# Turning the last 128 output columns of two matmuls in three of four token chunks

## The chip, the cores and the metric

One core of one Trainium2 chip. The metric is the device time of one execution in microseconds, here the median of three runs.

## The reference, cut to what matters

Two branches read the same x (2048 tokens of 640 features): a linear attention A and an MLP mixer B. They are mixed with a gate per token.

```python
o = num / den                                   # linear attention, 32 heads of 20
a = o.reshape(B, S, D) @ wo
x1 = x + hs                                     # hs: first MLP, shifted over tokens, @ w2
h2 = gelu(layernorm(x1) @ w3) @ w4              # w3: 640 x 1728, w4: 1728 x 640
b = x1 + h2
g = sigmoid((x * gate_w).sum(-1, keepdims=True))
return g * a + (1 - g) * b
```

With wo folded into the attention's key-value matrix (M, 640 x 640), the last stage is, for each token, g times (scaled query @ M), plus (1 - g) times (x1 + h @ w4), with h the result of the gelu.

## The kernel before, in words

The tokens are 16 tiles of 128 and four chunks of 512. The first stages make queries, keys, the gate, the key-value matrix M, and the first MLP (x_tok then holds x1). The last stages, around the change, are:

- **w3** (w3_group): per chunk 13 groups of 128 hidden features; each is five matmuls with 512 tokens moving into one bank of PSUM, and one gelu on ScalarE into h2T. The last 64 of the 1728 hidden features (w3_half) go to h2h, on partitions 0 to 63 for the even tiles and 64 to 127 for the odd.
- **attention tile** (a_tile, lines 1071 to 1080): POOL writes (1 - g) times x_tok of a tile into a slot of abx (four slots); TensorE multiplies the tile's scaled query, stationary, by M, moving: five matmuls of 512 output columns into one bank and five of 128 into the next; VectorE adds g times that to abx.
- **w4** per chunk: w4_half (lines 1084 to 1106) opens the accumulation with the 64 left hidden features, for the four tiles of the chunk at once, each pair of tiles side by side on the two halves of the array's rows. w4_tile (lines 1108 to 1131) then adds 13 matmuls of 512 columns and 13 of 128 per tile, with a 128 x 128 block of h2T stationary each time. VectorE then adds (1 - g) times PSUM to abx and writes x_tok: a 512-wide and a 128-wide instruction (both at line 652, the helper stt). out_tiles stores finished tiles.

PSUM has eight banks of 512 fp32 columns. `bank()` (line 527) picks one free bank, `pair()` (line 544) one of the four fixed pairs (0, 1), (2, 3), (4, 5), (6, 7) in which neither bank is held; each takes the one that its plan frees earliest. w4_half holds six banks, three whole pairs: four for the tiles' 512 columns and two for their tails. A bank leaves the hold when its tile's last group has been recorded.

The order of the work on each engine is made when the kernel is built: a planner (`_Items.run`, line 349) takes items from streams, each with a duration, dependencies and lags, and records the operations of the item that may start first. Every recorded operation waits on semaphores for the reads and writes before it (`_Sched.op`, line 216). So the order of instructions is fixed and what happens at run time is only waiting. Near the change the plan puts attention tile t + 4 behind w4 tile t, the w3 groups of the next chunk but one behind the four tiles, and the query scaling of tiles 12 to 15 on VectorE into chunk 0. Helpers record most operations, so many instructions have one line: L613 is a matmul group, L635 a multiply by a scalar, L652 a sum of a scaled input, L669 an activation, L282 a transposing DMA on SP.

Of the kernel before, what the change touches and what calls it, by code (L numbers as in the profile page):

```python
# [5 lines left out]
BF16 = mybir.dt.bfloat16  # L6
F32 = mybir.dt.float32
ACTF = mybir.ActivationFunctionType
ALU = mybir.AluOpType
# [41 lines left out]
class _Sched:  # L51
# [161 lines left out]
            if any(r.lo < 0 for r in lst):  # L213
                self.recs[space] = [r for r in lst if r.lo >= 0]

    def op(self, eng, fn, reads=(), writes=(), deps=(), cost=500.0):
        d, touched, newrecs, banks = self._collect(eng, reads, writes)
        d.extend(deps)
        waits = self._waits(eng, d)
        self.cnt[eng] += 1  # L220
        sem = "c:" + eng
        vc = dict(self.know[eng])
        ev = _Ev(sem, self.cnt[eng], vc)
        self._commit(ev, touched, newrecs, banks, eng)
        self.prog[eng].append((waits, fn, sem))
        self.seq.append((eng, waits, cost, sem, ev.val, 0))
        self.oplog.append((eng, ev.val, self.cur_item, waits))
        self.stats["ops"] += 1
        self.stats["waits"] += len(waits)
        return ev  # L230
# [199 lines left out]
def _build(nc, A_x, A_wqkv, A_wo, B_w1, B_w2, B_w3, B_w4, gate_w, out, dbg=None, stop=None):  # L430
# [113 lines left out]
    def pair():  # L544
        best = None
        for k_ in range(4):
            q_ = (bank_rr[0] // 2 + k_) % 4
            tf = 0.0
            ok = True
            for b in (2 * q_, 2 * q_ + 1):  # L550
                if b in bank_pend or b in bank_hold:
                    ok = False
                lk = sch.locks.get(b)
                if lk is not None:
                    tf = max(tf, sch.ev_time.get((lk[1].sem, lk[1].val), 1e18))
            if ok and (best is None or tf < best[0]):
                best = (tf, 2 * q_)
        b = best[1]
        bank_rr[0] = b + 2
        bank_pend.update((b, b + 1))  # L560
        return b
# [8 lines left out]
    def nfree(ap):  # L570
        n = 1
        for d_ in ap.shape[1:]:
            n *= d_
        return n
# [20 lines left out]
            cost = 150.0 + 1.2 * n  # L595
        return sch.op("pool", fn, reads, writes, cost=cost)

    def pe(fn, reads, writes, cost=500.0):
        for w_ in writes:
            sp_, rl = sch.rects(w_)  # L600
            if sp_ == "ps":
                for (_p0, _p1, lo, hi) in rl:
                    for b in range(lo // PS_BANK, (hi - 1) // PS_BANK + 1):
                        bank_pend.discard(b)
        return sch.op("pe", fn, reads, writes, cost=cost)

    def mm_group(out_ap, pairs, reads_extra=()):
        n = len(pairs)

        def fn(e, out_ap=out_ap, pairs=pairs, n=n):  # L610
            ins = None
            for i, (l, r) in enumerate(pairs):
                ins = e.matmul(out_ap, l, r, start=(i == 0), stop=(i == n - 1))  # L613
            return ins
        reads = [a for p in pairs for a in p] + list(reads_extra)
        return pe(fn, reads, [out_ap], cost=n * (max(nfree(pairs[0][1]), 24) * 0.4167 + 2.5))
# [11 lines left out]
    def ts(engf, out_ap, in_ap, s1, s2, op0, op1, extra_reads=()):  # L628
        rd = [in_ap] + [a for a in (s1, s2) if not isinstance(a, (int, float)) and a is not None] + list(extra_reads)
        cost = None  # L630
        if engf is pool:
            cost = 190.0 + 1.15 * nfree(out_ap)
        elif in_ap.dtype == BF16 and out_ap.dtype == BF16 and not in_psum(in_ap):
            cost = 65.0 + nfree(out_ap) / 3.84
        return engf(lambda e: e.tensor_scalar(out_ap, in_ap, s1, s2, op0, op1), rd, [out_ap], cost=cost)  # L635
# [431 lines left out]
        sch.dma("sp", pqnT[:, :, 128 * t:128 * (t + 1)], pq_tok[:, t, :], "trn%d" % slot("trn", 4), transpose=True)  # L1067

    abx_slot = {}

    def a_tile(t):
        sa = slot("abx", 4)
        abx_slot[t] = sa
        tag_set("abx", sa, t)
        ts(pool, abx[:, sa, :], x_tok[:, t, :], stg[:, 3, t:t + 1], 0.0, ALU.mult, ALU.add)
        tok = slice(128 * t, 128 * (t + 1))
        b = pair()
        mm_group(ps[:, b, 0:512], [(pqnT[:, j, tok], M_sb[:, j, 0:512]) for j in range(KD)])
        mm_group(ps[:, b + 1, 0:128], [(pqnT[:, j, tok], M_sb[:, j, 512:D]) for j in range(KD)])
        stt(abx[:, sa, :], psf[:, 512 * b:512 * b + D], stg[:, 2, t:t + 1], abx[:, sa, :], ALU.mult, ALU.add)  # L1080

    w4_banks = {}

    def w4_half(t):
        sl = (t // 4) % 2
        tag_chk("h2T", sl, t // 4)
        b0, b2, bt = pair(), pair(), pair()
        tiles = [((b0, b2)[i // 2] + i % 2, bt + i % 2, 128 * (i // 2)) for i in range(4)]
        for i in range(4):
            w4_banks[t + i] = tiles[i]  # L1090
        bank_hold.update((b0, b0 + 1, b2, b2 + 1, bt, bt + 1))

        def fn(e):
            ins = None
            for pr in range(2):
                for par, tail in ((0, False), (1, False), (0, True), (1, True)):
                    rows = slice(64 * par, 64 * par + 64)
                    bm, bs, q0 = tiles[2 * pr + par]
                    l = h2h[rows, t // 4, 128 * pr:128 * (pr + 1)]
                    if tail:  # L1100
                        ins = e.matmul(ps[:, bs, q0:q0 + 128], l, w4[rows, KFF, 512:D], start=(pr == 0), stop=False,  # L1101
                                       skip_group_check=True)
                    else:
                        ins = e.matmul(ps[:, bm, :], l, w4[rows, KFF, 0:512], start=True, stop=False)  # L1104
            return ins
        pe(fn, [h2h[:, t // 4, :], w4[:, KFF, :]], [ps[:, b, :] for b in (b0, b0 + 1, b2, b2 + 1, bt, bt + 1)], cost=760.0)

    def w4_tile(t):
        sa = abx_slot[t]
        tag_chk("abx", sa, t)  # L1110
        sl = (t // 4) % 2
        tag_chk("h2T", sl, t // 4)
        a = t % 4
        b1, b2, q0 = w4_banks.pop(t)

        def grp(o, n0, n1):
            prs = [(h2T[:, sl, k, 128 * a:128 * (a + 1)], w4[:, k, n0:n1]) for k in range(KFF)]

            def fn(e):
                ins = None  # L1120
                for i, (l, r) in enumerate(prs):
                    ins = e.matmul(o, l, r, start=False, stop=(i == KFF - 1), skip_group_check=(n0 > 0))  # L1122
                return ins
            pe(fn, [x_ for p_ in prs for x_ in p_], [o], cost=KFF * ((n1 - n0) * 0.4167 + 2.5))
        grp(ps[:, b1, 0:512], 0, 512)
        grp(ps[:, b2, q0:q0 + 128], 512, D)
        bank_hold.discard(b1)
        if a >= 2:
            bank_hold.discard(b2)
        stt(x_tok[:, t, 0:512], ps[:, b1, 0:512], stg[:, 3, t:t + 1], abx[:, sa, 0:512], ALU.mult, ALU.add)  # L1130
        stt(x_tok[:, t, 512:D], ps[:, b2, q0:q0 + 128], stg[:, 3, t:t + 1], abx[:, sa, 512:D], ALU.mult, ALU.add)

    def out_tiles(t0, t1):
        dst = out[0, 128 * t0:128 * t1, :].rearrange("(n p) d -> p n d", p=128)
        for n0, n1 in ((0, 512), (512, D)) if t0 == NT - 1 else ((0, D),):
            sch.dma("act" if n1 == 512 else "sp", dst[:, :, n0:n1], x_tok[:, t0:t1, n0:n1], "out%d" % slot("out", 4))
# [75 lines left out]
    for t in range(NT):  # L1212
        c = t // 4
        deps = [(("qt", t), 3.0), (("w4load",), 0.0), (("m", KD - 1), 1.0), (("mt",), 2.5)]
        if t >= 4:
            deps.append((("w4", t - 4), 0.3))
        else:
            deps.append((("w3", 1, t + 6), 0.0))
        IT.add("AT", ("a", t), 1.33, lambda t=t: a_tile(t), deps)
        deps4 = [(("a", t), 0.0), (("w3h", c - c % 2), GEL), (("w3", c, KFF - 1), GEL)]  # L1220
        if t % 4 == 0:
            deps4.append((("w3", min(c + 1, NCH - 1), KFF - 1), 0.0))
            if t == 0:
                deps4.append((("a", 3), 0.0))
        elif t + 3 < NT:
            deps4.append((("a", t + 3), 0.0))
        if t % 4 == 0:
            IT.add("W4", ("w4h", t), 0.76, lambda t=t: w4_half(t), deps=deps4)
        IT.add("W4", ("w4", t), 3.5, lambda t=t: w4_tile(t), deps=deps4)
        if t in OUT_AT:  # L1230
            IT.add("OUT", ("out", t), 0.0, lambda t=t: out_tiles(OUT_AT[t], t + 1), deps=[(("w4", t), 0.0)])

    hook = None
    if stop == "A":
# [45 lines left out]
```

## Time and profile before

| | us |
|---|---|
| median of three runs | 263.59 (263.54 to 263.64) |
| the profiled execution | 263.69 |
| its span, first to last instruction | 261.6 |
| TensorE busy in it | 256.0 |
| VectorE | 149.0 |
| ScalarE | 106.8 |
| POOL | 95.3 |

In the rows of the profile PE is TensorE's matmuls, PEld its weight loads, DVE VectorE, ACT ScalarE, SPq the DMA instructions of SyncE. A grouped row gives line, engine, operation, output<-input, shapes and count, then busy us, the mean ns of one, and the idle time ahead of them with what ended it. A row of the timeline gives start, length, engine and what ran, with a count where equal ones follow each other. A matmul's length runs from its start to its modelled end and overlaps the next; the distance between starts is the pace. Of a matmul's two inputs the moving one is named first; w stands for w1, w2, w3 and w4 alike, ps for all of PSUM.

### The profile page before, as it was taken

The numbers are of one execution on the slowest core, as the hardware profiler recorded it, in microseconds if no ns is written. First come the engines' busy times: TensorE is split into PE (matmuls) and PEld (weight loads), VectorE is DVE, ScalarE is ACT, GpSimd is POOL, SyncE is SP. The second block draws the span as 40 slices with busy tenths as digits, with TensorE's granted clock in tenths as the row PEclk, the third lists the DMA queues.
The fourth block names the chain that finished last, engine by engine and source line by source line (L and its number), as shares of the span: only waits on it lengthen the run. The fifth ranks groups of instructions, "written<-read, shape, count | busy, mean of one in ns | idle before, by whom it ended". The sixth has DMA issues, their size and how long they took to land.

```text
span 261.6 us, 4268 instructions
## 1 busy us (share of the span) xinstructions
PE 256.0 (98%) x1668; PEld 135.7 (52%) x1699; DVE 149.0 (57%) x267; ACT 106.8 (41%) x215; POOL 95.3 (36%) x150
## 2 busy tenths in 40 slices
PE   8999999999999999999999999999999999999996
PEld 4555555555555555554444545554455544455553
DVE  2497787899903699979995407992023410143332
ACT  1386767752355756684875140005500045100000
POOL 5003996849774018687753201230011100011000
PEclk9999999999999999999999999999999999999999
DMA  6885979660566895544766600232000020000211
GB/s 198 253 91 137 165 172 172 179 122 16 87 125 103 224 387 155 76 81 74 111 124 125 103 0 0 41 84 77 0 3 0 3 100 0 3 0 0 103 50 50
DMA packets 50612, 24.82 MB, mean 95 GB/s; under 512 B 41973, under 2 KB 49182, under 8 KB 50593
## 3 DMA queue, kind: packets, MB, share of 16 engines
q1 hardware_dynamic: 49152, 20.98, 36.6%
q0 software_dynamic: 1152, 3.28, 5.7%
q8 instruction: 13, 0.21, 0.3%
q10 hardware_dynamic: 288, 0.30, 0.3%
q14 instruction: 7, 0.05, 0.1%
HBM read 12.04 MB, written 2.62 MB: 56 GB/s over the span
## 4 chain that ended last, share of the span: by engine, by line
PE 95%; DVE 1%; DMA 1%; issue 1%; ACT 0%
PE ps L613 60%; PE ps L1122 21%; PE ps L795 8%; PE ps L874 2%; DMA x_tok<-in_A_x_dram 1%; PE ps L1036 1%; PE ps L1104 1%; DVE x_tok L652 1%; PE ps L875 1%; PE ps L624 1%; PE ps L950 1%; DVE abx L652 0%; ACT junk L668 0%; DVE xT L678 0%; PE ps L1101 0%
## 5 line engine op out<-in xcount | busy, mean ns | idle before, releaser
L613 PE MATMUL ps<-xnT,w 128*128 128x512 bf16 x348 | 80.7, 379 | 0.7 <-issue 0.2
L1122 PE MATMUL ps<-w,h2T 128*128 128x512 bf16 (+1 forms) x411 | 58.1, 298 | 0.3
L669 ACT ACTIVATE h2T<-ps 128x512 bf16<-128x512 f32 x52 | 30.4, 600 | 65.7 <-PE ps L613 65.7
L613 PEld LDWEIGHTS ps<-xnT,w 128*128 128x128 bf16 x360 | 34.0, 98 | 36.9 <-issue 0.4
L652 DVE SCALAR_TENSOR_TENSOR x_tok<-ps,stg,abx 128x512 bf16<-128x512 f32 (+1 forms) x32 | 17.2, 550 | 61.6 <-PE ps L1122 61.6
L635 POOL TENSOR_SCALAR abx<-x_tok,stg 128x640 f32<-128x640 bf16 x16 | 14.8, 927 | 101.9 <-DVE x_tok L652 95.1
L1122 PEld LDWEIGHTS ps<-w,h2T 128*128 128x128 bf16 x416 | 32.4, 98 | 25.6 <-issue 1.1
L635 POOL TENSOR_SCALAR xn<-x_tok,st 128x640 bf16<-128x640 bf16 x32 | 33.8, 1062 | 15.3 <-DMA xnT<-xn 14.8
L669 ACT ACTIVATE Er<-ps 128x640 bf16<-128x640 f32 x32 | 22.3, 705 | 18.7 <-PE ps L875 8.6
L668 ACT ACTIVATE junk<-x_tok 128x640 bf16<-128x640 bf16 x32 | 23.6, 737 | 4.8 <-DVE x_tok L650 4.3
L669 ACT ACTIVATE hsT<-ps 128x512 bf16<-128x512 f32 (+1 forms) x32 | 18.9, 594 | 15.1 <-PE ps L613 14.8
L613 PE MATMUL ps<-M_sb,pqnT 128*128 128x512 bf16 (+1 forms) x157 | 23.7, 297 | 0.2
L613 PE MATMUL ps<-w,hsT 128*128 128x128 bf16 (+1 forms) x158 | 23.7, 298 | 0.1
L795 PE MATMUL ps<-pk_tok,x_tok 128*128 128x128 bf16 (+1 forms) x156 | 23.3, 297 | 0.2
L652 DVE SCALAR_TENSOR_TENSOR abx<-ps,stg,abx 128x640 f32<-128x640 f32 x16 | 14.1, 884 | 14.6 <-PE ps L613 14.6
L613 PE MATMUL ps<-wkg,xT 128*128 128x131 bf16 (+1 forms) x148 | 22.4, 298 | 0.1
L613 PEld LDWEIGHTS ps<-w,hsT 128*128 128x128 bf16 x160 | 13.3, 98 | 12.3
L613 PEld LDWEIGHTS ps<-M_sb,pqnT 128*128 128x128 bf16 x160 | 13.1, 98 | 10.4
L613 PE MATMUL ps<-wq,xT 128*128 128x128 bf16 (+1 forms) x118 | 18.1, 298 | 0.1
L650 DVE SCALAR_TENSOR_TENSOR x_tok<-ps,x_tok 128x640 bf16<-128x640 f32 x16 | 13.1, 821 | 6.9 <-PE ps L613 6.0
L613 PEld LDWEIGHTS ps<-wkg,xT 128*128 128x128 bf16 x150 | 12.2, 98 | 9.0
L795 PEld LDWEIGHTS ps<-pk_tok,x_tok 128*128 128x128 bf16 x160 | 12.4, 98 | 8.4
(70 smaller groups left out, 231.8 us busy)
## 6 DMA issues: line engine op xcount, KB each, us to landing
w<-in_B_w_dram SPq DMA_DIRECT2D x1, 2160.0 KB, 8.5
w<-in_B_w_dram SPq DMA_DIRECT2D x1, 2080.0 KB, 14.1
x_tok<-in_A_x_dram SPq DMA_DIRECT2D x3, 640.0 KB, 5.8
out_dram<-x_tok SPq DMA_DIRECT2D x3, 640.0 KB, 3.5
w<-in_B_w_dram POOLq DMA_DIRECT2D x8, 160.0 KB, 5.1
wkg<-in_A_wqkv_dram SPq DMA_DIRECT2D x5, 160.0 KB, 4.1
wv<-in_A_wqkv_dram POOLq DMA_DIRECT2D x1, 800.0 KB, 6.2
wo_aug<-in_A_wo_dram POOLq DMA_DIRECT2D x5, 150.0 KB, 5.2
```

The source lines that it names most:

```text
L613: ins = e.matmul(out_ap, l, r, start=(i == 0), stop=(i == n - 1))
L624: ins = e.transpose(o, s_, ident[:])
L635: return engf(lambda e: e.tensor_scalar(out_ap, in_ap, s1, s2, op0, op1), rd, [out_ap], cost=cost)
L650: return dve(lambda e: e.scalar_tensor_tensor(out_ap, in0, scalar, in1, op0, op1, accum_out=accum), rd, [out_ap, accum], cost=cost + 70.0)
L652: return dve(lambda e: e.scalar_tensor_tensor(out_ap, in0, scalar, in1, op0, op1), rd, [out_ap], cost=cost)
L668: return act(lambda e: e.activation(out_ap, in_ap, func, bias=bias, scale=scale, accum_out=accum), rd, wr, cost=cost)
L669: return act(lambda e: e.activation(out_ap, in_ap, func, bias=bias, scale=scale), rd, wr, cost=cost)
L795: ins = e.matmul(o, l, r, start=(t0 + q_ == 0), stop=(t0 + q_ == NT - 1))
L874: e.matmul(ps[:, b, 0:512], l, w[:, k, 0:512], start=(k == 0), stop=(k == KD - 1))
L875: return e.matmul(ps[:, b + 1, 0:n2], l, w[:, k, 512:512 + n2], start=(k == 0), stop=(k == KD - 1))
L950: ins = e.matmul(o, l, r_, start=st_, stop=sp_, skip_group_check=True)
L1122: ins = e.matmul(o, l, r, start=False, stop=(i == KFF - 1), skip_group_check=(n0 > 0))
```

## The change

For tiles 0 to 11 (chunks 0 to 2; `TURNED` is 12) the last 128 of the 640 output columns are computed turned: the weights are stationary and 512 tokens move, so one bank gets 128 features by 512 tokens. This is done for the attention output (a_tail, one group of five matmuls per chunk) and for w4 (w4_tail, one group of 13 per chunk, ahead of the chunk's four tiles). ScalarE copies each turned bank to tlT in bf16, a transposing DMA on SP turns it back into tl, and tail_sum on VectorE makes, per chunk, one 512-wide sum of the w4 part and x1, and per tile a multiply of the attention part by g and a sum with (1 - g). POOL's and VectorE's abx instructions become 512 wide for these tiles. Chunk 3 is as before.

w4_half holds five single banks in these chunks: four for the tiles and one for the turned tail, which the two row halves write in turn; the second of its matmuls waits for the first through the new argument `after`. The attention tiles 0 to 11 take a single bank, tiles 12 to 15 a pair as before.

```diff
-    def op(self, eng, fn, reads=(), writes=(), deps=(), cost=500.0):
+    def op(self, eng, fn, reads=(), writes=(), deps=(), cost=500.0, after=None):
...
+        if after is not None:
+            waits.append((after.sem, after.val))
...
+    tlT = rb.alloc("tlT", [128, 2, 512], BF16)
+    tl = rb.alloc("tl", [128, 2, 4, 128], BF16)
+    tlu = rb.alloc("tlu", [128, 4, 128], F32)
+    tlv = rb.alloc("tlv", [128, 1, 128], F32)
...
+    TURNED = NT - 4
     def a_tile(t):
...
-        ts(pool, abx[:, sa, :], x_tok[:, t, :], stg[:, 3, t:t + 1], 0.0, ALU.mult, ALU.add)
+        n = 512 if t < TURNED else D
+        ts(pool, abx[:, sa, 0:n], x_tok[:, t, 0:n], stg[:, 3, t:t + 1], 0.0, ALU.mult, ALU.add)
-        b = pair()
+        b = bank() if t < TURNED else pair()
         mm_group(ps[:, b, 0:512], [(pqnT[:, j, tok], M_sb[:, j, 0:512]) for j in range(KD)])
-        mm_group(ps[:, b + 1, 0:128], [(pqnT[:, j, tok], M_sb[:, j, 512:D]) for j in range(KD)])
+        if t >= TURNED:
+            mm_group(ps[:, b + 1, 0:128], [(pqnT[:, j, tok], M_sb[:, j, 512:D]) for j in range(KD)])
...
+    def turn(b, i):
+        activation(tlT[:, i, :], ps[:, b, :], ACTF.Copy)
+        sch.dma("sp", tl[:, i, :, :], tlT[:, i, :], "tl%d" % i, transpose=True)
+    def a_tail(c):
+        b = bank()
+        mm_group(ps[:, b, :], [(M_sb[:, j, 512:D], pqnT[:, j, 512 * c:512 * (c + 1)]) for j in range(KD)])
+        turn(b, 0)
+    def tail_sum(c):
+        xt = x_tok[:, 4 * c:4 * c + 4, 512:D]
+        tt(dve, tlu[:, :, :], tl[:, 1, :, :], xt, ALU.add)
+        for i in range(4):
+            t = 4 * c + i
+            ts(dve, tlv[:, 0, :], tl[:, 0, i, :], stg[:, 2, t:t + 1], 0.0, ALU.mult, ALU.add)
+            stt(x_tok[:, t, 512:D], tlu[:, i, :], stg[:, 3, t:t + 1], tlv[:, 0, :], ALU.mult, ALU.add)
     def w4_half(t):
...
-        b0, b2, bt = pair(), pair(), pair()
+        turned = t < TURNED
+        if turned:
+            bs = [bank() for _ in range(5)]
+            tiles = [(bs[i], bs[4], 128 * i) for i in range(4)]
+        else:
+            b0, b2, bt = pair(), pair(), pair()
...
+        def tail_t(e, par):
+            rows = slice(64 * par, 64 * par + 64)
+            o = ps[:, bs[4], :].rearrange("p (n h q) -> p n h q", h=2, q=128)[:, :, par, :]
+            return e.matmul(o, w4[rows, KFF, 512:D], h2h[rows, t // 4, :].rearrange("p (n q) -> p n q", q=128),
+                            start=(par == 1), stop=False, skip_group_check=True)
...
+        first = pe(lambda e: tail_t(e, 1), rd, [ps[:, bs[4], :]], cost=60.0)
+        pe(fn, rd, [ps[:, b, :] for b in bs[:4]], cost=540.0)
+        pe(lambda e: tail_t(e, 0), rd, [ps[:, bs[4], :]], cost=110.0, after=first)
...
+    def w4_tail(c):
+        b = w4_banks[4 * c][1]
+        w4_acc(ps[:, b, :], [(w4[:, k, 512:D], h2T[:, c % 2, k, :]) for k in range(KFF)], True)
+        bank_hold.discard(b)
+        turn(b, 1)
     def w4_tile(t):
...
-        grp(ps[:, b1, 0:512], 0, 512)
-        grp(ps[:, b2, q0:q0 + 128], 512, D)
+        w4_acc(ps[:, b1, :], [(hs[k], w4[:, k, 0:512]) for k in range(KFF)], False)
         bank_hold.discard(b1)
+        if t >= TURNED:
+            w4_acc(ps[:, b2, q0:q0 + 128], [(hs[k], w4[:, k, 512:D]) for k in range(KFF)], True)
...
-        stt(x_tok[:, t, 512:D], ps[:, b2, q0:q0 + 128], stg[:, 3, t:t + 1], abx[:, sa, 512:D], ALU.mult, ALU.add)
+        if t >= TURNED:
+            stt(x_tok[:, t, 512:D], ps[:, b2, q0:q0 + 128], stg[:, 3, t:t + 1], abx[:, sa, 512:D], ALU.mult, ALU.add)
...
-        IT.add("AT", ("a", t), 1.33, lambda t=t: a_tile(t), deps)
+        IT.add("AT", ("a", t), 1.08 if t < TURNED else 1.33, lambda t=t: a_tile(t), deps)
+        if t % 4 == 3 and t < TURNED:
+            IT.add("AT", ("at", c), 1.08, lambda c=c: a_tail(c), [(("qt", t), 3.0)] + ([(("ts", c - 1), 0.0)] if c else []))
...
+            if t < TURNED:
+                IT.add("W4", ("w4t", c), 2.8, lambda c=c: w4_tail(c), deps=[(("at", c), 0.0)])
-        IT.add("W4", ("w4", t), 3.5, lambda t=t: w4_tile(t), deps=deps4)
+        IT.add("W4", ("w4", t), 2.8 if t < TURNED else 3.5, lambda t=t: w4_tile(t), deps=deps4)
+        if t % 4 == 2 and t < TURNED:
+            IT.add("TS", ("ts", c), 0.0, lambda c=c: tail_sum(c), deps=[(("w4", t), 0.0), (("at", c), 4.0)])
```

w4_acc is the accumulation loop that was inside w4_tile; the order of the four mains in a turned w4_half is upper and lower rows in turn. The stores of chunks 0 to 2 also wait for tail_sum.

On the engines this gives: TensorE 54 matmuls of 512 columns in place of 216 of 128 columns, and in each of the first three w4_half six matmuls in place of eight; VectorE 27 instructions more and 12 fewer; ScalarE six copies; SP six transposes, of which two stand ahead of the query transposes of tiles 12 to 14.

More of the change, by code (lines that the diff above doesn't have):

```diff
@@ L596, in pool, with pe @@
         return sch.op("pool", fn, reads, writes, cost=cost)
-    def pe(fn, reads, writes, cost=500.0):
+    def pe(fn, reads, writes, cost=500.0, after=None):
         for w_ in writes:
@@ L604, in pe @@
                         bank_pend.discard(b)
-        return sch.op("pe", fn, reads, writes, cost=cost)
+        return sch.op("pe", fn, reads, writes, cost=cost, after=after)
     def mm_group(out_ap, pairs, reads_extra=()):
@@ L1074, in a_tile @@
         tag_set("abx", sa, t)
-        ts(pool, abx[:, sa, :], x_tok[:, t, :], stg[:, 3, t:t + 1], 0.0, ALU.mult, ALU.add)
+        n = 512 if t < TURNED else D
+        ts(pool, abx[:, sa, 0:n], x_tok[:, t, 0:n], stg[:, 3, t:t + 1], 0.0, ALU.mult, ALU.add)
         tok = slice(128 * t, 128 * (t + 1))
-        b = pair()
+        b = bank() if t < TURNED else pair()
         mm_group(ps[:, b, 0:512], [(pqnT[:, j, tok], M_sb[:, j, 0:512]) for j in range(KD)])
-        mm_group(ps[:, b + 1, 0:128], [(pqnT[:, j, tok], M_sb[:, j, 512:D]) for j in range(KD)])
-        stt(abx[:, sa, :], psf[:, 512 * b:512 * b + D], stg[:, 2, t:t + 1], abx[:, sa, :], ALU.mult, ALU.add)
+        if t >= TURNED:
+            mm_group(ps[:, b + 1, 0:128], [(pqnT[:, j, tok], M_sb[:, j, 512:D]) for j in range(KD)])
+        stt(abx[:, sa, 0:n], psf[:, 512 * b:512 * b + n], stg[:, 2, t:t + 1], abx[:, sa, 0:n], ALU.mult, ALU.add)
+    def turn(b, i):
[12 more added lines that the diff above has]
+            stt(x_tok[:, t, 512:D], tlu[:, i, :], stg[:, 3, t:t + 1], tlv[:, 0, :], ALU.mult, ALU.add)
     w4_banks = {}
@@ L1086, in w4_half @@
         tag_chk("h2T", sl, t // 4)
-        b0, b2, bt = pair(), pair(), pair()
-        tiles = [((b0, b2)[i // 2] + i % 2, bt + i % 2, 128 * (i // 2)) for i in range(4)]
+        turned = t < TURNED
[4 more added lines that the diff above has]
+            b0, b2, bt = pair(), pair(), pair()
+            bs = [b0, b0 + 1, b2, b2 + 1, bt, bt + 1]
+            tiles = [((b0, b2)[i // 2] + i % 2, bt + i % 2, 128 * (i // 2)) for i in range(4)]
@@ L1089, in w4_half, with main, tail @@
         for i in range(4):
             w4_banks[t + i] = tiles[i]
-        bank_hold.update((b0, b0 + 1, b2, b2 + 1, bt, bt + 1))
+        bank_hold.update(bs)
+        def main(e, pr, par):
+            rows = slice(64 * par, 64 * par + 64)
+            bm, bs, q0 = tiles[2 * pr + par]
+            return e.matmul(ps[:, bm, :], h2h[rows, t // 4, 128 * pr:128 * (pr + 1)], w4[rows, KFF, 0:512], start=True, stop=False)
+        def tail(e, pr, par):
+            rows = slice(64 * par, 64 * par + 64)
+            bm, bs, q0 = tiles[2 * pr + par]
+            return e.matmul(ps[:, bs, q0:q0 + 128], h2h[rows, t // 4, 128 * pr:128 * (pr + 1)], w4[rows, KFF, 512:D],
+                            start=(pr == 0), stop=False, skip_group_check=True)
@@ L1093, in fn @@
+        def tail_t(e, par):
+            rows = slice(64 * par, 64 * par + 64)
+            o = ps[:, bs[4], :].rearrange("p (n h q) -> p n h q", h=2, q=128)[:, :, par, :]
+            return e.matmul(o, w4[rows, KFF, 512:D], h2h[rows, t // 4, :].rearrange("p (n q) -> p n q", q=128),
+                            start=(par == 1), stop=False, skip_group_check=True)
         def fn(e):
             ins = None
+            if turned:
+                for i in range(4):
+                    ins = main(e, i // 2, i % 2)
+                return ins
@@ L1095, in fn @@
             for pr in range(2):
[L1096 to L1104, printed above, removed]
@@ L1105, in fn @@
-            return ins
-        pe(fn, [h2h[:, t // 4, :], w4[:, KFF, :]], [ps[:, b, :] for b in (b0, b0 + 1, b2, b2 + 1, bt, bt + 1)], cost=760.0)
+                for par, piece in ((0, main), (1, main), (0, tail), (1, tail)):
+                    ins = piece(e, pr, par)
+            return ins
+        rd = [h2h[:, t // 4, :], w4[:, KFF, :]]
+        if not turned:
+            pe(fn, rd, [ps[:, b, :] for b in bs], cost=760.0)
+            return
+        first = pe(lambda e: tail_t(e, 1), rd, [ps[:, bs[4], :]], cost=60.0)
@@ new lines, in w4_half, with w4_acc, fn @@
+        pe(fn, rd, [ps[:, b, :] for b in bs[:4]], cost=540.0)
+        pe(lambda e: tail_t(e, 0), rd, [ps[:, bs[4], :]], cost=110.0, after=first)
+    def w4_acc(o, prs, shared):
+        def fn(e):
+            ins = None
+            for i, (l, r) in enumerate(prs):
+                ins = e.matmul(o, l, r, start=False, stop=(i == KFF - 1), skip_group_check=shared)
+            return ins
+        pe(fn, [x_ for p_ in prs for x_ in p_], [o], cost=KFF * (nfree(o) * 0.4167 + 2.5))
+    def w4_tail(c):
+        tag_chk("h2T", c % 2, c)
+        b = w4_banks[4 * c][1]
+        w4_acc(ps[:, b, :], [(w4[:, k, 512:D], h2T[:, c % 2, k, :]) for k in range(KFF)], True)
+        bank_hold.discard(b)
+        turn(b, 1)
@@ L1114, in w4_tile @@
         b1, b2, q0 = w4_banks.pop(t)
[L1116 to L1124, printed above, removed]
-        grp(ps[:, b1, 0:512], 0, 512)
-        grp(ps[:, b2, q0:q0 + 128], 512, D)
+        hs = [h2T[:, sl, k, 128 * a:128 * (a + 1)] for k in range(KFF)]
+        w4_acc(ps[:, b1, :], [(hs[k], w4[:, k, 0:512]) for k in range(KFF)], False)
         bank_hold.discard(b1)
-        if a >= 2:
-            bank_hold.discard(b2)
+        if t >= TURNED:
+            w4_acc(ps[:, b2, q0:q0 + 128], [(hs[k], w4[:, k, 512:D]) for k in range(KFF)], True)
+            if a >= 2:
+                bank_hold.discard(b2)
         stt(x_tok[:, t, 0:512], ps[:, b1, 0:512], stg[:, 3, t:t + 1], abx[:, sa, 0:512], ALU.mult, ALU.add)
-        stt(x_tok[:, t, 512:D], ps[:, b2, q0:q0 + 128], stg[:, 3, t:t + 1], abx[:, sa, 512:D], ALU.mult, ALU.add)
+        if t >= TURNED:
+            stt(x_tok[:, t, 512:D], ps[:, b2, q0:q0 + 128], stg[:, 3, t:t + 1], abx[:, sa, 512:D], ALU.mult, ALU.add)
     def out_tiles(t0, t1):
@@ L1228, in _build @@
             IT.add("W4", ("w4h", t), 0.76, lambda t=t: w4_half(t), deps=deps4)
-        IT.add("W4", ("w4", t), 3.5, lambda t=t: w4_tile(t), deps=deps4)
+            if t < TURNED:
[3 more added lines that the diff above has]
+            IT.add("TS", ("ts", c), 0.0, lambda c=c: tail_sum(c), deps=[(("w4", t), 0.0), (("at", c), 4.0)])
         if t in OUT_AT:
-            IT.add("OUT", ("out", t), 0.0, lambda t=t: out_tiles(OUT_AT[t], t + 1), deps=[(("w4", t), 0.0)])
+            IT.add("OUT", ("out", t), 0.0, lambda t=t: out_tiles(OUT_AT[t], t + 1), deps=[(("w4", t), 0.0)] + ([(("ts", c), 0.0)] if t < TURNED else []))
     hook = None
```

## The prediction

> **What bounds the kernel now.** I read the page's busy shares first, then the chain that ended last by line, then the clock.
>
> ```profile
> span 261.6 us, 4268 instructions
> PE 256.0 (98%) x1668; PEld 135.7 (52%) x1699; DVE 149.0 (57%) x267; ACT 106.8 (41%) x215; POOL 95.3 (36%) x150
> ...
> PEclk9999999999999999999999999999999999999999
> ...
> PE 95%; DVE 1%; DMA 1%; issue 1%; ACT 0%
> PE ps L613 60%; PE ps L1122 21%; PE ps L795 8%; PE ps L874 2%; DMA x_tok<-in_A_x_dram 1%; PE ps L1036 1%; PE ps L1104 1%; DVE x_tok L652 1%; PE ps L875 1%; PE ps L624 1%; PE ps L950 1%; DVE abx L652 0%; ACT junk L668 0%; DVE xT L678 0%; PE ps L1101 0%
> ```
>
> TensorE is busy 98% at full clock and 95% of the chain is its own work. So only two things count: the time TensorE takes for the same columns, and any new moment at which it waits. VectorE, ScalarE and the queues have slack (57% and 41% busy); they count only where TensorE waits for a bank that they empty.
>
> How fast columns stream I read from the timeline of TensorE in chunk 1, with the eviction of each w3 group on ScalarE as a clock.
>
> ```profile
> 189.93 3.71 PE L1122 MATMUL ps<-w,h2T 128*128 128x512 bf16 x26
> ...
> 209.50 14.19 PE L613 MATMUL ps<-xnT,w 128*128 128x512 bf16 x63
> ```
>
> ```profile
> 210.78 0.60 ACT L669 ACTIVATE h2T<-ps 128x512 bf16<-128x512 f32 x1 [20.80 <-PE ps L613]
> ...
> 223.73 0.60 ACT L669 ACTIVATE h2T<-ps 128x512 bf16<-128x512 f32 x1 [0.48 <-PE ps L613]
> ```
>
> Twelve w3 groups of five matmuls lie between the two evictions: 12.95 us / 60 = **215.8 ns** for 512 columns. From 189.93 to 209.50 run four w4 tiles and four attention tiles, 72 matmuls of 512 and 72 of 128 columns: 19.57 - 72 x 0.2158 = 4.03 us, or **56.0 ns** for 128 columns. A quarter of a wide one is 53.95 ns. So the narrow tails lose 2.05 ns each, and nothing else: the weight load (98 ns, a row below) is hidden behind them.
>
> **The change, part by part.**
>
> *Turned tails.* In twelve tiles 13 + 5 = 18 tail matmuls of 128 columns go, 216 in all; 54 of 512 come. 216 x 56.0 = 12.10 us against 54 x 215.8 = 11.65 us: **-0.44 us**. That is the whole gain on TensorE, since the columns streamed are as many as before.
>
> *The half contraction (w4_half).* Before, eight matmuls on two 64-row halves; now six: a turned tail of 256 columns on the upper half, four mains, a turned tail on the lower half.
>
> ```profile
> 223.63 0.39 PE L1104 MATMUL ps<-w,h2h 64*128 64x512 bf16 x2
> 223.85 0.22 PE L1101 MATMUL ps<-w,h2h 64*128 64x128 bf16 x2
> 223.91 0.38 PE L1104 MATMUL ps<-w,h2h 64*128 64x512 bf16 x2
> 224.13 0.22 PE L1101 MATMUL ps<-w,h2h 64*128 64x128 bf16 x2
> 224.28 0.39 PE L1122 MATMUL ps<-w,h2T 128*128 128x512 bf16 x1
> ```
>
> The halves run side by side (two mains of 512 columns in 0.22 us), and each half still streams 1280 columns: 0.65 us as before. The last turned tail now waits for the first. That one starts at 0, streams 0.11 us, and a matmul ends about 0.16 us after its streaming (379 ns against 215.8), so it is done near 0.27 us; the waiting one is due at 0.44 us. Queued behind it is only TensorE's own next group. I take 0; the bounds are -0.1 (less switching, three times 0.03) and +0.3 us (three times 0.1).
>
> *Evictions and transposes.* Six ScalarE copies and six crossbar transposes are added.
>
> ```profile
> L669 ACT ACTIVATE h2T<-ps 128x512 bf16<-128x512 f32 x52 | 30.4, 600 | 65.7 <-PE ps L613 65.7
> ```
>
> ```profile
> pqnT<-pq_tok SPq DMA_TRANSPOSE x16, 2.6
> ```
>
> A copy costs about 0.60 us in gaps of 0.48 us and more between evictions. On SP the new transposes stand ahead of the transposes of tiles 12 to 15 and of output stores, each about 2.6 us to land. The first user, tail_sum, comes behind three w4 tiles (over 8 us) after the second copy; tiles 12 to 15 are used a chunk and a half later. Cost 0; if that cover were gone, each late transpose would hold VectorE, not TensorE.
>
> *VectorE.* The prices by shape, and how close dependent ones follow each other:
>
> ```profile
> L652 DVE SCALAR_TENSOR_TENSOR abx<-ps,stg,abx 128x640 f32<-128x640 f32 x16 | 14.1, 884 | 14.6 <-PE ps L613 14.6
> L643 DVE TENSOR_TENSOR qprod<-pq_tok,zb 128x640 f32<-128x640 bf16 x16 | 13.0, 815 | 0.0
> L652 DVE SCALAR_TENSOR_TENSOR x_tok<-ps,stg,abx 128x512 bf16<-128x512 f32 x16 | 12.0, 750 | 61.6 <-PE ps L1122 61.6
> L635 DVE TENSOR_SCALAR Er<-Er 128x640 bf16<-128x640 bf16 x32 | 11.8, 369 | 8.6 <-ACT Er L669 8.5
> L652 DVE SCALAR_TENSOR_TENSOR x_tok<-ps,stg,abx 128x128 bf16<-128x128 f32 x16 | 5.6, 350 | 0.0
> L635 DVE TENSOR_SCALAR dnr<-dnr 128x32 f32<-128x32 f32 x16 | 3.9, 244 | 0.1
> L1063 DVE TENSOR_TENSOR pq_tok<-pq_tok,dnr 128x40 bf16<-128x40 bf16 x16 | 3.1, 191 | 0.0
> ```
>
> ```profile
> 161.99 0.17 DVE L635 TENSOR_SCALAR dnr<-dnr 128x32 f32<-128x32 f32 x1
> 162.19 0.35 DVE L1054 RECIPROCAL dnr<-dnr 128x32 f32<-128x32 f32 x1
> 162.58 0.89 DVE L1063 TENSOR_TENSOR pq_tok<-pq_tok,dnr 128x600 bf16<-128x600 bf16 x2
> ```
>
> From 512 to 128 columns an x_tok sum falls 400 ns, 1.04 ns an element. The 640-element qprod at 815 then gives the 512-wide tlu 0.68 us. No row shows the 128-wide multiply into tlv (between the 32-wide 0.17 and the 640-wide 0.37; I take 0.27) nor the all-SBUF sum (between 0.19 and 0.35; I take 0.30). The four pairs depend on each other through one tlv buffer, with 0.03 us between dependent ones. One tail_sum: 0.68 + 4 x (0.27 + 0.03 + 0.30 + 0.03) = **3.2 us**, bounds 2.3 and 3.8.
>
> In chunk 0 this comes on top of the query scaling:
>
> ```profile
> 155.00:175.00 20.00, 19.89 (x149) 11.12 (x151) 16.02 (x30) 0.60 (x1) 4.47 (x4) 1.00 0.12 23
> ```
>
> VectorE (the third busy column) has 16.0 of these 20 us; 3.2 come, 1.9 go (four tail sums of 0.35, four abx narrower by 0.13), and it starts about 2.8 us later because the turned tail group runs ahead of the first w4 tile. So it ends the chunk some 4 us later than now. But the banks that it then still holds are taken by the next w3 groups one after the other, 1.08 us apart, and by the instruction list the tightest (the sixth group, on the bank of abx of tile 6) still has about 3 us. Chunk 1 has no scaling. I take no wait in either.
>
> *Banks, chunk 2.* Here is the cost. Before, w4_half held three whole bank pairs and an attention tile always had the fourth. Now it holds five single banks; in the changed program's instruction list, chunk 2 has the mains in 2, 4, 0, 7 and the tail in 6. Attention tiles 12 to 15 are not turned and still need a pair, and each of the four pairs has a held bank. The only one that opens is (2, 3), when w4 tile 8 has finished in bank 2. So tile 12's first matmul, directly behind tile 8's last, waits until VectorE has read bank 2. Everything on TensorE is queued behind it. The same kind of wait stands in the trace, ahead of the last w4_half:
>
> ```profile
> 238.96 3.69 PE L1122 MATMUL ps<-w,h2T 128*128 128x512 bf16 x26
> ...
> 241.97 1.08 DVE L652 SCALAR_TENSOR_TENSOR x_tok<-ps,stg,abx 128x512 bf16<-128x512 f32 x2 [1.92 <-PE ps L1122]
> 242.77 0.10 PEld L1104 LDWEIGHTS ps<-w,h2h 64*128 64x128 bf16 x2 [0.29 <-DVE x_tok L652]
> ```
>
> Tile 11's last wide matmul starts at 238.96 + 12 x 0.2158 = 241.55; VectorE starts 0.42 us later, takes 0.75 and TensorE goes on 0.05 after: 1.22 us from that start instead of 0.22. Tile 12 waits **+1.0 us** (bounds 0.98 and 1.1, the latter with 0.1 of weight load bared).
>
> *The last w4_half (tile 12).* It now takes the pairs (2, 3), (4, 5), (0, 1), and so waits for the sum abx of tile 14, which stands on VectorE behind tail_sum of chunk 2. Counted from the start of tile 10's last wide matmul: VectorE 0.42, x_tok 0.73 until the next starts (1.08 for the two, less 0.35), tail_sum 3.2, abx 0.88, back to TensorE 0.05, together 5.28 us. TensorE gets there after 0.22 + 1.36 (attention tile 14, five wide and five narrow) + 2.81 (13 wide) = 4.38 us. It waits 0.90 where it now waits 0.28 (242.77 less 242.49, the due time: 238.96 + 13 x (0.2158 + 0.0560)): **+0.6 us**. With tail_sum at 2.3 us nothing is late and only the change of row halves remains (0.1 of the 0.28): -0.2. At 3.8 us it is +1.2.
>
> *POOL* only gets shorter (512 for 640 columns). The last chunk and the end of the kernel are unchanged.
>
> Sum: -0.44 + 0 + 1.0 + 0.6 = **+1.2 us**, a span of 262.8. The profiled execution took 263.69 us, 2.09 outside its span, so 264.9; the median of the three runs is 0.1 lower: **264.8 us**.
>
> **The rivals.**
>
> *One wait only.* If tail_sum is as short as 2.3 us, the second wait goes: -0.44 + 1.0 - 0.2 = +0.4 us, **264.0**. For it: scalar operations on 32 elements run in 0.17 us. Against: 350 ns for the only 128-wide sum. [...]
>
> *The other side, faster.* If the narrow matmuls were paced by their weight loads, turning would save far more than the waits cost.
>
> ```profile
> L1122 PEld LDWEIGHTS ps<-w,h2T 128*128 128x128 bf16 x416 | 32.4, 98 | 25.6 <-issue 1.1
> ```
>
> At 98 ns each, 216 would take 21.2 us against 11.65: -9.5 + 1.6 = **255.7 us**. It decides from a narrow pace of (11.65 + 1.6 + 0.5) / 216 = 64 ns on; the trace says 56.0, so I give it little. [...]
>
> *More waits.* If the wait of a matmul on an earlier one costs its upper bound and tail_sum too: -0.4 + 1.1 + 1.2 + 0.3 = +2.2 us, **265.8**. For it: 32-wide scalar operations that took far more than their 0.17 us.
>
> ```profile
> 120.78 0.78 DVE L635 TENSOR_SCALAR dnr<-dnr 128x32 f32<-128x32 f32 x1
> ...
> 138.10 0.66 DVE L635 TENSOR_SCALAR dnr<-dnr 128x32 f32<-128x32 f32 x1
> ```
>
> That the change doesn't do what it says is excluded: the instruction list has the turned matmuls, copies and transposes.
>
> **How the numbers follow.** Forecast 0.72; one wait 0.13; more waits 0.10; faster 0.05. A measurement of this kernel tells about 0.2% (0.53 us) from no change. Slower by more than that (above 264.1): the forecast and more waits, 0.82. Within: one wait, 0.13. Faster: 0.05. The range, from the sum's low ends (-0.44 - 0.1 + 0.98 - 0.2 = +0.24, 263.8) to most of the high ones, is 263.8 to 265.6.
>
> **What would show it.** Right: in the waits, an attention matmul behind VectorE's x_tok once for about 1.0 us near 230 us, and the last w4_half behind VectorE's abx for about 0.9 us; 54 more wide matmuls at 215.8 ns, none narrow in chunks 0 to 2; tail_sum near 3.2 us. Wrong: no wait at tile 12 (its pair was free), waits inside the first three w4_half, or TensorE waiting for banks in the w3 groups of chunks 2 or 3.

## The result, and the profile after

The changed kernel takes 265.07 us (median of 13 runs) against 263.62 us for the kernel before (13 runs beside them): a ratio of 1.0049 with a 95% interval of 1.0029 to 1.007. That is slower, by 0.3 to 0.7%, and 0.3 us above the forecast of 264.8. One of the 13 runs had a lower granted clock (0.994, 269.73 us) and is left out of the ratio.

In the changed kernel's lines the numbers are six higher ahead of w4 (L619 is a matmul group, L641 a multiply by a scalar, L649 a tensor sum, L658 the scaled sum, L675 an activation). In w4_half L1128 are the mains, L1139 the turned tails, L1133 chunk 3's narrow tails; L1164 is the accumulation of w4. The page of the changed kernel:

```profile
span 264.5 us, 3968 instructions
PE 256.1 (97%) x1502; PEld 128.7 (49%) x1531; DVE 152.6 (58%) x282; ACT 110.4 (42%) x221; POOL 95.1 (36%) x150
...
PEclk9999999999999999999999999999999999999999
```

The clock is full, as before (mean 1.000 in both traces). The page counts 166 matmuls fewer (the weight loads 168; some matmul records are missing from both traces), and the busy time is the same within 0.1 us, so it doesn't show the gain. What counts is where matmuls start late. The waits of TensorE's matmuls (engine, output, line, what it waited for, us in total, times, longest):

```profile
PE ps L1128 <- DVE abx L658: 1.3, 1, 1.3
PE ps L619 <- DVE x_tok L658: 0.9, 1, 0.9
...
PE ps L619 <- DMA xT<-x_tok: 0.7, 1, 0.7
```

The first two are the waits that the prediction named, each there once. The third lies near 46 us, in a stage that the change doesn't touch. The profiled execution (266.2 us) has it, and its first w4_half starts at 155.91 us where the kernel before has 154.94. So the two traces are compared from the first w4_half on. TensorE around the two waits:

```profile
224.32 0.28 PE L1139 MATMUL ps<-h2h,w 64*128 64x256 bf16 x1
224.33 0.71 PE L1128 MATMUL ps<-w,h2h 64*128 64x512 bf16 x4
224.77 0.27 PE L1139 MATMUL ps<-h2h,w 64*128 64x256 bf16 x1
224.97 2.76 PE L1164 MATMUL ps<-h2T,w 128*128 128x512 bf16 x12
227.79 2.97 PE L1164 MATMUL ps<-w,h2T 128*128 128x512 bf16 x13
231.69 1.52 PE L619 MATMUL ps<-M_sb,pqnT 128*128 128x512 bf16 x10 [0.94 <-DVE x_tok L658]
233.05 2.97 PE L1164 MATMUL ps<-w,h2T 128*128 128x512 bf16 x13
235.85 1.52 PE L619 MATMUL ps<-M_sb,pqnT 128*128 128x512 bf16 x10
237.21 2.97 PE L1164 MATMUL ps<-w,h2T 128*128 128x512 bf16 x12
...
241.38 2.97 PE L1164 MATMUL ps<-w,h2T 128*128 128x512 bf16 x13
245.68 0.39 PE L1128 MATMUL ps<-w,h2h 64*128 64x512 bf16 x2 [1.33 <-DVE abx L658]
```

Read the starts. Thirteen wide matmuls take 2.80 us (233.05 to 235.85), the old pace. (The group of 12 at 237.21 takes as long; one record of it is missing.) Tile 8's accumulation starts at 227.79, so tile 12's attention matmul was due at 230.59 and starts at 231.69: **1.10 us** late. (The bracket says 0.94 because it counts from the modelled end of the matmul before, 227.79 + 2.97 = 230.76.) The accumulation that starts at 241.38 ends its issue at 244.18, and the last w4_half starts at 245.68: **1.50 us** late, of which the kernel before already had 0.28. VectorE between them:

```profile
240.22 0.75 DVE L658 SCALAR_TENSOR_TENSOR x_tok<-ps,stg,abx 128x512 bf16<-128x512 f32 x1 [1.53 <-PE ps L1164]
240.88 0.68 DVE L649 TENSOR_TENSOR tlu<-tl,x_tok 128x512 f32<-128x512 bf16 x1
241.48 0.83 DVE L641 TENSOR_SCALAR tlv<-tl,stg 128x128 f32<-128x128 bf16 x1
242.35 0.35 DVE L658 SCALAR_TENSOR_TENSOR x_tok<-tlu,stg,tlv 128x128 bf16<-128x128 f32 x1
242.74 0.29 DVE L641 TENSOR_SCALAR tlv<-tl,stg 128x128 f32<-128x128 bf16 x1
...
244.47 0.35 DVE L658 SCALAR_TENSOR_TENSOR x_tok<-tlu,stg,tlv 128x128 bf16<-128x128 f32 x1
244.74 0.88 DVE L658 SCALAR_TENSOR_TENSOR abx<-ps,stg,abx 128x640 f32<-128x640 f32 x1
```

The chain to the last w4_half is here in full. The sum abx at 244.74 empties the pair that w4_half wants, and in front of it stands tail_sum of chunk 2, 240.88 to 244.74: **3.86 us** where 3.2 were priced. One row doesn't fit the others: the first multiply into tlv takes 0.83 us, the later ones 0.29. POOL at that time:

```profile
236.90 0.80 POOL L641 TENSOR_SCALAR abx<-x_tok,stg 128x640 f32<-128x640 bf16 x1 [4.46 <-DVE x_tok L658]
241.06 1.17 POOL L641 TENSOR_SCALAR abx<-x_tok,stg 128x640 f32<-128x640 bf16 x1 [3.36 <-DVE x_tok L658]
```

POOL's multiply for abx of tile 14 is issued while tlu runs, and takes 1.17 us instead of its usual 0.80; VectorE's multiply, issued 0.42 us after POOL's, takes 0.54 more. Here both took longer: POOL's multiply starts 0.18 us into tlu and ends at 242.23, VectorE's ends at 242.31. In chunk 0 it goes otherwise: POOL's multiply starts 0.42 us ahead of VectorE's there too, but VectorE's takes its usual 0.28 us (last section). What decides between the two isn't shown.

From the first w4_half to the end of the span the kernel before takes 261.6 - 154.94 = 106.7 us and the changed one 264.5 - 155.91 = 108.6: 1.9 more, which is 1.10 + (1.50 - 0.28) less about 0.4 of pace.

### The profile page after: what moved, and what is told of

Its sections match the earlier page's. It is cut to its first block, busy times and chain, and to the rows that moved or that the text cites. A ratio compares the mean times of both kernels' runs of the same rounds, so it can differ in the third digit from the quotient of the medians.

```text
span 264.5 us, 3968 instructions
## 1 busy us (share of the span) xinstructions
PE 256.1 (97%) x1502; PEld 128.7 (49%) x1531; DVE 152.6 (58%) x282; ACT 110.4 (42%) x221; POOL 95.1 (36%) x150
## 4 chain that ended last, share of the span: by engine, by line
PE 73%; DMA 10%; DVE 7%; SPq 7%; issue 2%; ACT 0%
PE ps L619 47%; PE ps L1164 17%; PE ps L801 7%; DMA x_tok<-in_A_x_dram 7%; SPq L284 5%; DMA xT<-x_tok 3%; DVE x_tok L658 3%; SPq L288 2%; DVE tlv L641 1%; DVE abx L658 1%; PE ps L1042 1%; PE ps L1128 1%; DVE pq_tok L1069 1%; DVE qprod L649 1%; PE ps L956 1%
## 5 line engine op out<-in xcount | busy, mean ns | idle before, releaser
L619 PE MATMUL ps<-xnT,w 128*128 128x512 bf16 x350 | 80.9, 379 | 0.6 <-issue 0.2
L619 PEld LDWEIGHTS ps<-xnT,w 128*128 128x128 bf16 x360 | 34.2, 98 | 38.4 <-ACT h2h L675 0.4
L641 POOL TENSOR_SCALAR abx<-x_tok,stg 128x512 f32<-128x512 bf16 (+1 forms) x16 | 14.2, 892 | 103.2 <-DVE x_tok L658 103.2
L1164 PE MATMUL ps<-w,h2T 128*128 128x512 bf16 (+1 forms) x254 | 49.8, 346 | 0.4
L658 DVE SCALAR_TENSOR_TENSOR x_tok<-ps,stg,abx 128x512 bf16<-128x512 f32 (+1 forms) x20 | 13.3, 669 | 61.0 <-PE ps L1164 61.0
L641 POOL TENSOR_SCALAR xn<-x_tok,st 128x640 bf16<-128x640 bf16 x32 | 34.5, 1085 | 16.5 <-DMA xnT<-xn 16.1
L675 ACT ACTIVATE h2T<-ps 128x512 bf16<-128x512 f32 x52 | 30.5, 600 | 22.9 <-PE ps L619 22.9
L1164 PEld LDWEIGHTS ps<-w,h2T 128*128 128x128 bf16 x260 | 23.1, 98 | 24.1 <-issue 0.3
L675 ACT ACTIVATE Er<-ps 128x640 bf16<-128x640 f32 x32 | 22.3, 705 | 19.6 <-PE ps L619 9.5
L675 ACT ACTIVATE hsT<-ps 128x512 bf16<-128x512 f32 (+1 forms) x32 | 18.9, 594 | 15.1 <-PE ps L619 14.8
L619 PE MATMUL ps<-w,hsT 128*128 128x128 bf16 (+1 forms) x158 | 23.7, 298 | 0.1
L619 PE MATMUL ps<-wkg,xT 128*128 128x131 bf16 (+1 forms) x148 | 22.4, 298 | 0.1
L619 PE MATMUL ps<-M_sb,pqnT 128*128 128x512 bf16 (+1 forms) x99 | 20.8, 347 | 0.9 <-DVE x_tok L658 0.9
L675 ACT ACTIVATE tlT<-ps 128x512 bf16<-128x512 f32 x6 | 3.6, 597 | 42.5 <-PE ps L619 33.6
L658 DVE SCALAR_TENSOR_TENSOR abx<-ps,stg,abx 128x512 f32<-128x512 f32 (+1 forms) x16 | 12.5, 781 | 12.4 <-PE ps L619 8.7
L619 PEld LDWEIGHTS ps<-w,hsT 128*128 128x128 bf16 x160 | 13.3, 98 | 12.3
L619 PE MATMUL ps<-wq,xT 128*128 128x128 bf16 (+1 forms) x118 | 18.2, 298 | 0.8 <-DMA xT<-x_tok 0.7
L641 DVE TENSOR_SCALAR Er<-Er 128x640 bf16<-128x640 bf16 x32 | 11.2, 350 | 10.1 <-ACT Er L675 9.8
L619 PEld LDWEIGHTS ps<-wkg,xT 128*128 128x128 bf16 x150 | 12.2, 97 | 9.0
```

Of the source, the lines that this page charges most:

```text
L658: return dve(lambda e: e.scalar_tensor_tensor(out_ap, in0, scalar, in1, op0, op1), rd, [out_ap], cost=cost)
L675: return act(lambda e: e.activation(out_ap, in_ap, func, bias=bias, scale=scale), rd, wr, cost=cost)
```

## The experiments

All four ran on one chip beside the kernel before (median 263.55 us of 25 runs). The theory: the change is worth about -0.4 us of pace, and two waits for banks, each made by one decision (five single banks; where tail_sum stands on VectorE), cost the rest. The rival: the added copies, transposes and VectorE work slow TensorE's stream, in which case the waits are a symptom and mending them doesn't bring the pace back.

### tail_sum of chunk 2 one tile later

```diff
-        if t % 4 == 2 and t < TURNED:
+        if t % 4 == (3 if c == 2 else 2) and t < TURNED:
             IT.add("TS", ("ts", c), 0.0, lambda c=c: tail_sum(c), ...
```

> The changed kernel with one edit: tail_sum of chunk 2 is recorded behind w4 tile 11 instead of tile 10, so that VectorE makes abx of tile 14 ahead of it. Theory (two bank waits): the last w4_half waits no more (1.5 us in the changed kernel's profile, 0.1 us of row change stays), the wait of tile 12 (1.1 us) stays; 263.7 to 264.1 us. Rival (the added copies, transposes and sums slow TensorE's own stream): about 265.1 as before the edit, with TensorE's pace above 215.8 ns.

Measured: 263.82 us (12 runs), a ratio to the kernel before of 1.0025 (1.0005 to 1.0044). The second wait is gone; the matmul waits that are left in the w4 stages are one:

```profile
PE ps L619 <- DVE x_tok L658: 0.9, 1, 0.9
```

```profile
240.76 2.97 PE L1164 MATMUL ps<-w,h2T 128*128 128x512 bf16 x13
243.66 0.39 PE L1128 MATMUL ps<-w,h2h 64*128 64x512 bf16 x2
```

The thirteenth matmul ends its issue at 243.56 and w4_half starts at 243.66; the 0.10 us stands at the change to matmuls on half the rows, and so it does ahead of the first w4_half of this trace (due at 155.19, start at 155.29). So this wait comes from tail_sum's place on VectorE, and the median is 1.25 us below the changed kernel's 265.07. The edit also takes tail_sum away from POOL's multiply (its first multiply takes 0.28 us here); what that alone is worth, the last run tells.

### w4_half of tile 8 on two whole pairs and one bank

```diff
         if turned:
-            bs = [bank() for _ in range(5)]
+            if t == 8:
+                b0, b2 = pair(), pair()
+                bs = [b0, b0 + 1, b2, b2 + 1, bank()]
+            else:
+                bs = [bank() for _ in range(5)]
```

> The changed kernel with one edit: in chunk 2 w4_half takes two whole pairs for the mains and one bank for the tail, so that a pair stays free for tile 12. Theory: the 1.1 us wait of tile 12 goes, the wait of the last w4_half stays at 1.0 to 1.5 us (it is counted from tile 10's end); 263.9 to 264.2 us. Rival (stream slowed): 265.1.

Measured: 264.00 us (11 runs), 1.002 (1.0009 to 1.0031). Now the first wait is gone and the second is left, 1.50 us as before (L1132 is L1128 here, four lines on):

```profile
PE ps L1132 <- DVE abx L658: 1.3, 1, 1.3
```

```profile
226.53 2.97 PE L1168 MATMUL ps<-w,h2T 128*128 128x512 bf16 x13
229.33 1.52 PE L619 MATMUL ps<-M_sb,pqnT 128*128 128x512 bf16 x10
```

Tile 12's attention matmul starts 2.80 us behind the first of tile 8, exactly at the pace. So holding five banks does leave a pair free, if they are taken as two pairs and one bank; taken singly they blocked all four pairs.

### Both edits

> Both edits: tail_sum of chunk 2 late and whole pairs in chunk 2. Theory: no wait is left, only the narrow tails' loss is gone: the kernel before less 0.44 and less the 0.2 that its last w4_half waits, 263.0 us, faster than the kernel before by 0.6. Rival (stream slowed by the added work): 264 or more, slower than the kernel before, with no wait to show for it.

Measured: 262.83 us (7 runs), 0.9971 (0.9951 to 0.999): **faster than the kernel before**. TensorE has no wait left from the first w4_half on:

```profile
154.65 0.28 PE L1143 MATMUL ps<-h2h,w 64*128 64x256 bf16 x1
```

```profile
239.02 2.97 PE L1168 MATMUL ps<-w,h2T 128*128 128x512 bf16 x13
241.93 0.39 PE L1132 MATMUL ps<-w,h2h 64*128 64x512 bf16 x2
```

The kernel before has these two points at

```profile
154.94 0.39 PE L1104 MATMUL ps<-w,h2h 64*128 64x512 bf16 x2
...
242.77 0.39 PE L1104 MATMUL ps<-w,h2h 64*128 64x512 bf16 x2
```

From the first w4_half to the last: 87.28 us against 87.83, that is -0.55. The old wait of 0.28 shrinks to 0.10, which is -0.18; the other -0.37 is the pace. The prediction gave -0.44 for all turned tails, of which 20 matmuls (0.04) lie ahead of the first w4_half: -0.40 in this stretch. (The medians differ by 0.7 us, more than this; the section on the terms comes back to that.) The rival falls: with the same copies, transposes and VectorE work in place, TensorE keeps its pace (thirteen wide matmuls in 2.81 us, 226.53 to 229.34).

### Five slots for abx

POOL's abx of tile 14 has to wait for the slot of tile 10; with a fifth slot it runs earlier, away from tail_sum. tlv changes its place in SBUF to make room.

```diff
-    abx = rb.alloc("abx", [128, 4, D], F32)
+    abx = rb.alloc("abx", [128, 5, D], F32)
...
-    tlv = rb.alloc("tlv", [128, 1, 128], F32)
+    tlv = pa.alloc("tlv", [128, 1, 128], F32)
...
-        sa = slot("abx", 4)
+        sa = slot("abx", 5)
```

> The changed kernel with five abx slots in place of four (tlv moved to make room), so that POOL multiplies tile 14 before tail_sum of chunk 2 and not beside it; TensorE's and VectorE's orders are unchanged. If the first multiply of that tail_sum took 0.83 us in place of 0.29 because POOL worked beside it: it takes 0.29, the last w4_half waits 1.0 in place of 1.5, 264.5 us. Rival (it waited for a transpose to land, or the length is chance): it stays at 0.83 or varies, 265.0.

Measured: 264.81 us (5 runs), 1.0042 (1.003 to 1.0054). POOL, VectorE and TensorE:

```profile
237.93 0.80 POOL L641 TENSOR_SCALAR abx<-x_tok,stg 128x640 f32<-128x640 bf16 x1 [1.08 <-DVE abx L658]
```

```profile
240.03 0.68 DVE L649 TENSOR_TENSOR tlu<-tl,x_tok 128x512 f32<-128x512 bf16 x1
240.63 0.28 DVE L641 TENSOR_SCALAR tlv<-tl,stg 128x128 f32<-128x128 bf16 x1
...
243.34 0.88 DVE L658 SCALAR_TENSOR_TENSOR abx<-ps,stg,abx 128x640 f32<-128x640 f32 x1
```

```profile
240.52 2.97 PE L1164 MATMUL ps<-w,h2T 128*128 128x512 bf16 x13
244.28 0.39 PE L1128 MATMUL ps<-w,h2h 64*128 64x512 bf16 x2 [0.79 <-DVE abx L658]
```

Apart, each engine takes its usual time: POOL 0.80, the first tlv 0.28, tail_sum 243.34 - 240.03 = 3.31 us. The last w4_half is due at 243.32 and starts at 244.28, 0.96 us late: 0.54 less than in the changed kernel. So 0.54 us of the second wait was VectorE and POOL meeting, and this wait comes out near the 0.90 that the prediction had for it. That tlv moved is not the reason: with both edits it stays in its old place, and there chunk 2's first multiply, with no POOL work beside it, also takes 0.28. Nor is it chance: in the run with whole pairs the two meet again, and again POOL takes 1.17 and the multiply 0.83. The time alone wouldn't show it, for 264.81 us is halfway between the 264.5 expected and the rival's 265.0, and its interval overlaps that of the changed kernel; the 0.54 rests on the traces. With both edits:

```profile
243.30 0.28 DVE L641 TENSOR_SCALAR tlv<-tl,stg 128x128 f32<-128x128 bf16 x1
```

### The terms together

The terms as read from the traces (pace -0.41; first wait +1.10; second wait less the 0.28 of before) against two measures of the whole: the ratio, taken of 263.55 us, and the median span of all runs less that of the kernel before (261.5 us, 25 runs).

| | pace | first wait | second wait | sum | by the ratio | by the span |
|---|---|---|---|---|---|---|
| the change | -0.41 | +1.10 | +1.22 | +1.9 | +1.3 (0.8 to 1.8) | +1.8 |
| tail_sum later | -0.41 | +1.10 | -0.18 | +0.5 | +0.7 (0.1 to 1.2) | +0.6 |
| whole pairs | -0.41 | 0 | +1.22 | +0.8 | +0.5 (0.2 to 0.8) | +0.8 |
| both | -0.41 | 0 | -0.18 | -0.6 | -0.8 (-1.3 to -0.3) | -0.4 |
| five slots | -0.41 | +1.10 | +0.68 | +1.4 | +1.1 (0.8 to 1.4) | +1.6 |

The signs agree throughout. By the spans the order agrees too, and each sum comes out within 0.2 us; by the ratio tail_sum later and whole pairs change places, with intervals that overlap. For the change itself the sum lies just above the interval of the ratio. The runs show where the two measures part: the time outside the span, 2.0 to 2.2 us in each of the 25 runs of the kernel before, is 1.7 to 1.8 us in every run of the five kernels with the change, some 0.35 us less. Why is open; no run tries it. So of the 0.7 us by which both edits beat the kernel before, the median spans show 0.4 (the terms give 0.6), and the rest lies outside the span.

## Why the prediction was right, step by step

**The narrow tails (-0.44).** Right: -0.37 from the first w4_half on by the trace with both edits, -0.41 with the 0.04 that the prediction has ahead of it, and no other part of the change disturbed the pace. The faster rival, in which weight loads pace the narrow matmuls, is out: turning 216 of them bought 0.4 us and not 9.5.

**w4_half (0).** Right. Turned, it starts at 224.32 and the next group at 224.97: 0.65 us, as long as before (223.63 to 224.28). The turned tail that waits for its twin finds it done.

**Evictions and transposes (0).** Right: tail_sum never waited for a transpose (VectorE is not idle ahead of any tlu), and no w3 group waited for a bank. The copies cost what the gelu of the same shape costs, 597 ns against 600:

```profile
L675 ACT ACTIVATE tlT<-ps 128x512 bf16<-128x512 f32 x6 | 3.6, 597 | 42.5 <-PE ps L619 33.6 <-PE ps L1164 5.9 <-remote 3.0
```

**Tile 12's attention matmul (+1.0, bounds 0.98 and 1.1).** Right, at the upper bound: 1.10. Tile 8's last wide matmul starts at 227.79 + 12 x 0.2158 = 230.38, and TensorE goes on 1.31 us later instead of 0.22:

```profile
230.79 0.75 DVE L658 SCALAR_TENSOR_TENSOR x_tok<-ps,stg,abx 128x512 bf16<-128x512 f32 x1 [18.97 <-PE ps L1164]
```

VectorE starts 0.41 after that matmul's start, takes 0.75, and 0.15 pass until the waiting matmul starts, where the prediction's row had 0.05. That it is the bared weight load, as the upper bound assumed, isn't shown: the load itself starts only at 231.66, 0.12 after VectorE and 0.03 ahead of its matmul.

**tail_sum (3.2, bounds 2.3 and 3.8) and the last w4_half (+0.6).** The mechanism was right and the size was off: tail_sum took 3.86 us, just above the upper bound, and the wait grew by 1.22 instead of 0.6. By groups:

```profile
L649 DVE TENSOR_TENSOR tlu<-tl,x_tok 128x512 f32<-128x512 bf16 x3 | 2.0, 680 | 0.0
```

```profile
L641 DVE TENSOR_SCALAR tlv<-tl,stg x12: 279/286/830, 172.3 to 244.2; 128x128 f32<-128x128 bf16 x12
L658 DVE SCALAR_TENSOR_TENSOR x_tok<-tlu,stg,tlv x12: 350/350/579, 172.6 to 244.5; 128x128 bf16<-128x128 f32 x12
```

(The second view gives the least, the median and the longest in ns.) tlu came as scaled from qprod, 0.68. The multiplies were 0.29 and not 0.27, the all-SBUF sums 0.35 and not 0.30: the nearest row, the 128-wide sum out of PSUM at 350, was the right price. With them the prediction's sum would be 3.5; the run with five slots has 3.3, since tail_sum's first and last instructions overlap their successors by 0.1 us each. The 0.54 on top is POOL. The step that failed is "POOL only gets shorter": its duration was weighed, and not that it can meet VectorE. The profile of before had the warning, in the 32-wide multiplies of 0.78 and 0.66 us that the prediction quoted and left without a cause. POOL's timeline of the kernel before has an instruction beside each:

```profile
119.77 2.61 POOL L635 TENSOR_SCALAR xn<-x_tok,st 128x640 bf16<-128x640 bf16 x3
...
137.84 0.88 POOL L635 TENSOR_SCALAR xn<-x_tok,st 128x640 bf16<-128x640 bf16 x1 [3.16 <-DMA xnT<-xn]
```

VectorE's multiply starts at 138.10, inside the second of them, and ends at 138.76, when POOL's has ended (138.72). A meeting doesn't stretch it each time: the 32-wide multiply at 131.59 takes 0.19 with POOL's multiplies beside it, and there POOL's three take 3.81 us instead of the 2.61 above.

**The one-wait rival (264.0).** It needed a tail_sum of 2.3 us, with 128-wide instructions hardly longer than the 32-wide multiply (0.17 us) and the 40-wide product (0.19) of the kernel before. No run shows them: the shortest 128-wide multiply takes 0.28 us, the shortest sum 0.35, and the shortest tail_sum of chunk 2 is 3.3 us (3.30 with tail_sum later, 3.31 with five slots).

**The range.** 265.07 lies within 263.8 to 265.6. The forecast of +1.2 had the first wait 0.1 too low and the second 0.6 too low: it gave a span of 262.8, and the median of the runs is 263.3. It also took over the 2.09 us outside the span unchanged, and that came to 1.7 to 1.8. The two errors have opposite signs, so that the time came within 0.3 us of the forecast is in part luck.

## What to carry to other kernels

When a kernel is bound by one engine, price a change by the moments at which that engine must wait for a bank, and follow each bank back through the queue of the engine that empties it: here work that VectorE had ample time for cost 1.2 us because it stood in front of one eviction, and moved behind that eviction it made TensorE wait for nothing. How a hold is taken counts as well as how much is held: five banks picked singly blocked all four pairs, while two pairs and a bank left one free. A change that loses can hold a gain: undo its waits one at a time before it is dropped; with both gone this one runs 0.3% faster than the kernel it started from, a part of which lies outside the span and has no known cause.

## What the runs showed of the hardware

VectorE and POOL stretched each other where they overlapped: a 128-wide multiply from 0.29 to 0.83 us, POOL's 640-wide one from 0.80 to 1.17, both back to their usual times when they were apart (five slots). In chunk 1 of the changed kernel's trace the first multiply pays as well, 0.72 us (at 205.62), with POOL's 512-wide one at 1.06 (205.20) instead of 0.70 (210.27); 0.72 is also the longest multiply into tlv in the traces with both edits and with five slots. It doesn't hit every pairing alike. In chunk 0 POOL's 512-wide multiply starts within tlu as well, but VectorE's multiply then takes its usual time and the sum behind it pays:

```profile
171.66 0.68 DVE L649 TENSOR_TENSOR tlu<-tl,x_tok 128x512 f32<-128x512 bf16 x1
172.26 0.28 DVE L641 TENSOR_SCALAR tlv<-tl,stg 128x128 f32<-128x128 bf16 x1
172.58 0.58 DVE L658 SCALAR_TENSOR_TENSOR x_tok<-tlu,stg,tlv 128x128 bf16<-128x128 f32 x1
```

```profile
171.84 1.18 POOL L641 TENSOR_SCALAR abx<-x_tok,stg 128x512 f32<-128x512 bf16 x1 [3.11 <-DVE x_tok L658]
```

Which of VectorE's instructions gets ahead of POOL in such a moment wasn't tried by itself.
